# Transfers over all rows and a finer spread of weight decoding in the transform stage of a Fourier-filter kernel

## The chip, the cores and the metric

The kernel runs on one core of one Trainium2 chip. The metric is device time in microseconds (us) for one execution of the whole program, from inputs in device memory to the output in device memory. A single core has five engines that matter here: TensorE (PE) with its weight loads (PEld), VectorE (DVE), ScalarE (ACT), GpSimd (POOL) and SyncE (SP), which only issues transfers.

## The reference

A block filters a sequence in the frequency domain and sends the result through two gated layers:

```python
def _attn_ref(x, filt_r, filt_i):          # x: (2, 3008, 256)
    X = np.fft.rfft(x, axis=1)
    F = (filt_r + 1j * filt_i)[None, :, :]
    return np.fft.irfft(X * F, n=x.shape[1], axis=1).astype(np.float32)

def _moe_ref(x, w_gate, w_val, w_out):      # 256 -> 1536 -> 256
    g = x @ w_gate
    silu = g * (1.0 / (1.0 + np.exp(-g)))
    return (silu * (x @ w_val) @ w_out).astype(np.float32)

def _moe2_ref(x, w_in, w_out):              # 256 -> 2048 -> 256
    h = x @ w_in
    g = h * np.clip(h + 3.0, 0.0, 6.0) / 6.0
    return (g @ w_out).astype(np.float32)
```

All weights come as float64. The kernel gets them as pairs of 32-bit words and decodes them on the chip.

## The kernel before, in words

**The transform stage.** The length 3008 is split as 47 x 64, so a Fourier transform is two small matrix products. The 256 channels of the two batches are cut into 16 steps of 32 channels (the loop `for k in range(N + 2)` with N = 16). In step k stand, in this order on PE:

- n1(k), line 417: the product over the 47 rows of the input, 64 small matmuls, out of the buffer `xin`, into two PSUM banks. ACT copies the result to `first` (line 422).
- back(k-2), line 458: 32 matmuls that bring the filtered spectrum of two steps ago back over the 64 rows. ACT copies the result to `turned` (line 463).
- n2(k), line 431: 32 matmuls on `first[k]` over the 64 rows. It can't start before the copy of line 422.

After n2(k) comes the filter product: four operations on DVE (line 444), then two subtractions and two additions on POOL (lines 109 and 112 are the helpers `minus` and `plus`). For the first eight steps POOL also flips signs in the filter (line 409). Steps 16 and 17 hold back(14), back(15) and the first block's way back to time (`to_time`, line 157). The main stage follows: its first matmul is `l1` (line 246).

**Transfers.** All of them are issued by SP, in the program's order: input loads of two steps (`load_x`, line 381, one for each of the two row halves), filter loads (`load_filter`, line 384), raw weights (`Decode`, line 179), stores of the spectrum to `d2` (line 467, every fourth step, one for each half of the 128 rows) and the loads of `g` out of `d2` (line 140). The input has two buffers (tag `xs`) of two steps each, so the load of steps k+3 and k+4 is issued once n1(k) has read its buffer.

**Decoding.** A block of weights is decoded by one operation on ACT (`start`, line 184), three on DVE (`leading`, lines 192, 193, 195), and three more (`rest`, lines 202, 203 and an addition, line 112). Then ACT casts the word to its high part (`high_gv`, line 482, or line 530) and DVE subtracts for the low part (`low_gv`, line 485). In the transform stage three such blocks are decoded, `dec[0]`, `dec[1]` and `both`; the steps at which each part runs are written out by hand in the chain `if k == 5: ... elif k == 13`. Every engine runs its instructions in the order in which the program issues them. An ACT operation of the decoding that waits therefore holds back the copy to `first` of the next step, and with it n2 of that step.

**The main stage** goes over blocks of up to 512 tokens through both layers. Weights of the first layer are decoded on the way.

Of the kernel before, what the change touches and what calls it, by code (L numbers as in the profile page):

```python
# [16 lines left out]
P = 128  # L17
B, S, D = 2, 3008, 256
N1, N2 = 47, 64
N1P = 48  # L20
NK = 24
COLS = 8 * NK
DFF1, DFF2 = 1536, 2048
# [37 lines left out]
def _matrices():  # L61
# [11 lines left out]
    m[:, :NK, FIN:FIN + N1] = w * np.cos(a.T)  # L73
    m[:, NK:2 * NK, FIN:FIN + N1] = -w * np.sin(a.T)
# [4 lines left out]
def fft_conv_glu_mlp(ctx: ExitStack, tc: tile.TileContext, x, filt, mats, sgn, w1, w2, out):  # L79
# [21 lines left out]
    d2 = [dram.tile([2 * NK, N2, D], F32, name=f"d2_{b}") for b in range(B)]  # L101
# [67 lines left out]
    class Decode:  # L169
# [16 lines left out]
        def leading(self):  # L186
            if self.w is None:
                self.w = self.pool.tile([P, self.n], F32, tag="ww", name="ww")
            v, a, wu = nc.vector, self.a, self.w.bitcast(U32)
            au, high = a.bitcast(U32), self.raw[:, :, 1]  # L190

            v.tensor_scalar(out=a, in0=a, scalar1=LEAST, scalar2=MOST, op0=ALU.max, op1=ALU.min)
            v.tensor_scalar(out=wu, in0=au, scalar1=3, scalar2=0x3FFFFFF8,
                            op0=ALU.logical_shift_left, op1=ALU.bitwise_and)
            v.scalar_tensor_tensor(out=wu, in0=high, scalar=0xC0000000, in1=wu,
                                   op0=ALU.bitwise_and, op1=ALU.bitwise_or)

        def rest(self, engine=None):
            v, a, w = nc.vector, self.a, self.w
            au, wu, low = a.bitcast(U32), w.bitcast(U32), self.raw[:, :, 0]  # L200

            v.tensor_scalar(out=au, in0=wu, scalar1=0xFF800000, scalar2=None, op0=ALU.bitwise_and)
            v.scalar_tensor_tensor(out=a, in0=low, scalar=2.0 ** -52, in1=a, op0=ALU.mult, op1=ALU.mult)  # L203
            plus(w, w, a, engine or nc.gpsimd)
# [157 lines left out]
    with tc.manual_schedule():  # L362
# [13 lines left out]
        def load_x(k, n):  # L376
# [73 lines left out]
        def back(k):  # L450
# [35 lines left out]

        gt, xsd = {}, {}
        for k in range(N + 2):
# [13 lines left out]
            if k == 5:  # L502
                load_gv(0)
            elif k == 6:
                load_gv(1)
                dec[0].start()
            elif k == 7:
                dec[0].leading()
            elif k == 8:
                dec[0].rest(nc.vector)  # L510
                high_gv(0)
                dec[1].start()
            elif k == 9:
                low_gv(0)
                both = Decode(None, w1[:, 0:2, 1024:], 512,
                              (words(side[:, 1024:2048]), side[:, 2048:2560], dec[0].a))
                dec[1].leading()
            elif k == 10:
                dec[1].rest(nc.vector)
                high_gv(1)  # L520
                both.start()
            elif k == 11:
                low_gv(1)
                both.leading()
            elif k == 12:
# [306 lines left out]
```

## Time and profile before

| | us |
|---|---|
| median of 3 runs | 1233.47 |
| lowest, highest | 1231.89, 1237.01 |
| the profiled execution's own time | 1232.24 |
| its span in the trace | 1230.5 |
| busy PE / PEld / DVE | 1177.9 / 1044.3 / 1006.1 |
| busy ACT / POOL | 606.0 / 161.0 |

The table is to be read with care: a share of busy time is an average over a short stage at the start, in which PE is often idle, and a long one after it, in which PE is nearly always busy. The trace has the instructions by engine and time, what each engine waited for, and the transfers.

### The profile page before, as it was taken

To read this page: it belongs to the slowest core of one execution; us is meant where nothing else is said; L and a number is where in the kernel's file an instruction comes from. 1 tells how busy PE (TensorE), PEld (TensorE's weight loads), DVE (VectorE), ACT (ScalarE), POOL (GpSimd) and SP (SyncE) were. 2 spreads that over 40 slices of the span, in tenths; PEclk is the share of its full clock that TensorE was granted. 3 is DMA by queue.
4 is the path that set the end of the run, shared out by engine and by line. 5 is a ranking of instruction groups with operands and counts; after the bars stand their busy time and mean duration, and the time that the engine had idled before them with its cause. 6 is when DMAs were issued, how large, how long until landed. Compare 5 with 4: busy or idle time off the path is not lost.

```text
span 1230.5 us, 22770 instructions
## 1 busy us (share of the span) xinstructions
PE 1177.9 (96%) x9544; PEld 1044.3 (85%) x9544; DVE 1006.1 (82%) x1565; ACT 606.0 (49%) x897; POOL 161.0 (13%) x166
## 2 busy tenths in 40 slices
PE   6667999999999999999999999999999999999997
PEld 5656778888889988888888989999899999999997
DVE  2355888666577888877888899999999999999997
ACT  2223444444334444444444556666666666666664
POOL 3433244000000222201122320000000000000000
PEclk9888999999999999999999999999999999999999
DMA  8775530110011323121210310110011001101000
GB/s 191 159 167 115 135 103 26 55 23 18 17 38 52 84 80 104 35 85 41 68 52 16 111 62 1 35 35 8 28 33 35 6 28 35 35 1 35 33 18 16
DMA packets 35031, 68.28 MB, mean 55 GB/s; under 512 B 2832, under 2 KB 18832, under 8 KB 34256
## 3 DMA queue, kind: packets, MB, share of 16 engines
q1 hardware_dynamic: 34928, 66.82, 19.8%
q8 instruction: 75, 1.23, 0.4%
q14 instruction: 28, 0.23, 0.1%
HBM read 44.53 MB, written 22.28 MB: 54 GB/s over the span
## 4 chain that ended last, share of the span: by engine, by line
PE 88%; DVE 5%; DMA 3%; issue 2%; ACT 1%; SPq 1%; DVEq 0%
PE gv L246 51%; PE a L255 31%; PE a L121 2%; DMA side<-w_in 2%; PE a L431 1%; PE gv L157 1%; PE gv L458 1%; DMA xin<-x_in 1%; DVE hs L109 1%; DVE us L444 1%; PE gv L417 1%; SPq L467 1%; DVE h L109 0%; DVE x L203 0%; DVE h L765 0%
## 5 line engine op out<-in xcount | busy, mean ns | idle before, releaser
L255 PEld LDWEIGHTS a<-hs,wall 128*128 128x128 f32 x3276 | 408.3, 189 | 14.1 <-issue 1.2
L255 PE MATMUL a<-hs,wall 128*128 128x256 f32 (+1 forms) x3276 | 414.2, 282 | 1.8 <-issue 0.8
L246 PE MATMUL gv<-xs,wall 128*128 128x512 f32 (+1 forms) x1728 | 407.4, 391 | 1.4 <-ACT xs L608 1.2
L246 PEld LDWEIGHTS gv<-xs,wall 128*128 128x128 f32 x1728 | 320.8, 188 | 67.4 <-ACT xs L608 1.3
L109 DVE TENSOR_TENSOR hs<-h,hs 128x768 fp32r<-128x768 f32 (+2 forms) x324 | 350.6, 1082 | 30.0 <-ACT hs L302 18.1
L246 PE MATMUL gv<-xs,wi 128*128 128x512 f32 (+1 forms) x1152 | 276.0, 388 | 0.0
L246 PEld LDWEIGHTS gv<-xs,wi 128*128 128x128 f32 x1152 | 210.0, 188 | 37.1 <-DVE xs L109 0.4
L313 ACT CAST hs<-h 128x1024 fp32r<-128x1024 f32 (+1 forms) x156 | 160.8, 1031 | 116.3 <-DVE h L109 116.1
L302 ACT CAST hs<-h 128x768 fp32r<-128x768 f32 (+1 forms) x156 | 128.1, 821 | 150.6 <-PE a L255 95.1
L109 DVE TENSOR_TENSOR h<-h 128x512 f32<-128x512 f32 (+3 forms) x312 | 185.4, 594 | 6.8
L615 DVE TENSOR_TENSOR h<-h,gv 128x512 f32<-128x512 f32 (+1 forms) x144 | 96.8, 673 | 62.2 <-PE gv L246 58.1
L764 ACT ACTIVATE h<-gv 128x512 f32<-128x512 f32 (+1 forms) x192 | 109.8, 589 | 69.1 <-PE gv L246 51.1
L765 DVE SCALAR_TENSOR_TENSOR h<-h,gv 128x512 f32<-128x512 f32 (+1 forms) x192 | 129.1, 672 | 15.4 <-ACT h L764 10.4
L599 ACT ACTIVATE h<-gv 128x512 f32<-128x512 f32 (+1 forms) x144 | 84.7, 588 | 85.7 <-PE gv L246 84.3
L444 DVE TENSOR_TENSOR us<-a,x 128x384 f32<-128x384 f32 x64 | 31.5, 550 | 62.7 <-PE a L431 60.4
L112 POOL TENSOR_TENSOR ww<-ww,wa 128x512 f32<-128x512 f32 x16 | 20.7, 1295 | 377.1 <-issue 194.6
L112 DVE TENSOR_TENSOR h<-h 128x256 f32<-128x256 f32 (+1 forms) x156 | 67.6, 433 | 2.1
L431 PE MATMUL a<-first,mat 64*64 64x192 f32 x512 | 33.4, 385 | 22.7 <-ACT first L422 22.7
L431 PEld LDWEIGHTS a<-first,mat 64*64 64x64 f32 x512 | 25.9, 160 | 26.8 <-ACT first L422 24.9
L121 PE MATMUL a<-hs,wall 128*128 128x512 f32 x144 | 36.9, 407 | 3.7 <-DVE hs L109 3.7
L121 PEld LDWEIGHTS a<-hs,wall 128*128 128x128 f32 x144 | 27.7, 193 | 11.1 <-DVE hs L109 4.6
L417 PE MATMUL gv<-mat,xin 48*64 48x48 f32 x1024 | 24.4, 236 | 11.6 <-issue 9.3
(93 smaller groups left out, 616.1 us busy)
## 6 DMA issues: line engine op xcount, KB each, us to landing
raw<-w_in SPq DMA_DIRECT2D x16, 512.0 KB, 4.2
x<-w_in SPq DMA_DIRECT2D x10, 768.0 KB, 4.0
d<-turned SPq DMA_DIRECT2D x8, 768.0 KB, 8.4
xin<-x_in SPq DMA_DIRECT2D x14, 384.0 KB, 9.1
yd<-y SPq DMA_DIRECT2D x10, 512.0 KB, 2.9
g<-yd SPq DMA_DIRECT2D x10, 512.0 KB, 3.9
y_out<-y SPq DMA_DIRECT2D x20, 256.0 KB, 2.3
wt<-wd SPq DMA_DIRECT2D x8, 448.0 KB, 3.4
```

What stands on the lines that cost most here:

```text
L109: (engine or nc.vector).tensor_tensor(out=out, in0=a, in1=b, op=ALU.subtract)
L112: (engine or nc.vector).tensor_tensor(out=out, in0=a, in1=b, op=ALU.add)
L121: nc.tensor.matmul(acc, w, v, start=first and i == 0, stop=last and i == 2)
L246: nc.tensor.matmul(acc[:, :n], w[:, r, k * P:(k + 1) * P], xs[:, v, k, :n], start=(r, v, k) == (0, 0, 0), stop=(r, k) == (1, 1))
L255: nc.tensor.matmul(acc[b][:, 256 * h:256 * h + nt], w[:, r, iw], hs[:, v, ih, :nt], start=first and h == 0 and v == 0 and r == 1, stop=las ...
L302: nc.scalar.copy(out=self.parts(0, 0, 3), in_=v(1, 4))
L313: nc.scalar.copy(out=self.parts(0, 3, 7), in_=self.values(4, 8))
L431: nc.tensor.matmul(accs[o][rows(r), part * COLS:(part + 1) * COLS].rearrange("p (c q) -> p c q", q=NK), mat[rows(o), w:w + N2], f[rows(o), ...
L599: nc.scalar.activation(out=h, in_=hid[p].halves(gate), func=AF.Silu)
L615: nc.vector.tensor_tensor(out=h, in0=h, in1=hid[p].halves(val), op=ALU.mult)
L764: nc.scalar.activation(out=h, in_=pre, func=AF.Relu, bias=3.0)
L765: nc.vector.scalar_tensor_tensor(out=h, in0=h, scalar=6.0, in1=pre, op0=ALU.min, op1=ALU.mult)
```

## The change

It has four parts. The input is laid out so that one load brings two steps of both row halves, over 112 rows (47 rows of data and one of zeros, 16 unused rows, 48 rows again), and the loads are issued on ACT's queue. The filter is laid out so that the load of one step is contiguous. The store to `d2` takes all 128 rows at once; the rows of `d2` are ordered otherwise, and two lines of the matrix constants follow. The decoding in the transform stage is cut into six parts a block, of which two are run in a step (from a table `todo`); the raw words are loaded at steps 3, 5 and 10 in place of 5, 6 and 9, and the last addition of a block runs on POOL in place of DVE.

```diff
+XR = 64 + N1P
...
-    m[:, :NK, FIN:FIN + N1] = w * np.cos(a.T)
-    m[:, NK:2 * NK, FIN:FIN + N1] = -w * np.sin(a.T)
+    m[:, 0:2 * NK:2, FIN:FIN + N1] = w * np.cos(a.T)
+    m[:, 1:2 * NK:2, FIN:FIN + N1] = -w * np.sin(a.T)
...
-    d2 = [dram.tile([2 * NK, N2, D], F32, name=f"d2_{b}") for b in range(B)]
+    d2 = [dram.tile([NK, P, D], F32, name=f"d2_{b}") for b in range(B)]
...
-            nc.sync.dma_start(out=g[rows(r, N1P), :t1 - t0], in_=d2[b][:, 32 * r + t0:32 * r + t1])
+            nc.sync.dma_start(out=g[rows(r, N1P), :t1 - t0],
+                              in_=d2[b].rearrange("q (h n) c -> (q h) n c", h=2)[:, 32 * r + t0:32 * r + t1])
...
+        def part(self, i, engine=None):
...
+            if i == 0:
+                v.tensor_scalar(out=a, in0=a, scalar1=LEAST, scalar2=MOST, op0=ALU.max, op1=ALU.min)
...
+            elif i == 4:
+                v.scalar_tensor_tensor(out=a, in0=low, scalar=2.0 ** -52, in1=a, op0=ALU.mult, op1=ALU.mult)
+            else:
+                plus(w, w, a, engine or nc.gpsimd)
...
-            for r in range(2):
-                nc.sync.dma_start(out=xin[k // 2][rows(r, N1P), k % 2:k % 2 + n], in_=x[b, r, :, j:j + n])
+            nc.scalar.dma_start(out=xin[k // 2][:XR, k % 2:k % 2 + n], in_=x[b, j // 2, :, j % 2:j % 2 + n])
...
-            nc.sync.dma_start(out=fl[:, j], in_=filt[:, j])
+            nc.sync.dma_start(out=fl[:, j], in_=filt[j])
...
-                for h in range(2):
-                    nc.sync.dma_start(out=d2[b][h * NK:(h + 1) * NK, :, a * P:(a + 1) * P].rearrange("q n c -> n q c"),
-                                      in_=turned[rows(h), a])
+                nc.sync.dma_start(out=d2[b][:, :, a * P:(a + 1) * P].rearrange("q p c -> p q c"), in_=turned[:, a])
...
+        def load_both():
+            dec["o"] = Decode(None, w1[:, 0:2, 1024:], 512, (words(side[:, 1024:2048]), side[:, 2048:2560], dec[0].a))
...
+        todo = {3: [lambda: load_gv(0)], 5: [lambda: load_gv(1)], 6: [lambda: dec[0].start()]}
+        k = 7
+        for f in (0, 1, "o"):
+            for i in (0, 2, 4):
+                todo.setdefault(k, []).extend([lambda f=f, i=i: dec[f].part(i), lambda f=f, i=i: dec[f].part(i + 1)])
+                k += 1
+            if f == "o":
+                todo[k - 1].append(high_o1)
+                todo[k] = [lambda: low_o1(0), lambda: low_o1(1)]
+            else:
+                todo[k - 1] += [lambda f=f: high_gv(f)]
+                todo[k] = [lambda f=f: low_gv(f)]
+                todo[k] += [load_both, lambda: dec[1].start()] if f == 0 else [lambda: dec["o"].start()]
...
-            if k == 5:
-                load_gv(0)
-            elif k == 6:
-                load_gv(1)
-                dec[0].start()
-            elif k == 7:
-                dec[0].leading()
-            elif k == 8:
-                dec[0].rest(nc.vector)
-                high_gv(0)
-                dec[1].start()
...
+            for step in todo.get(k, ()):
+                step()
+            if k == N - 4:
                 dec[2] = decode_w1(2)
                 gt[0] = load_g(0, 0)
...
-    xt = np.zeros((B, 2, N1P, 8, 1024), f32)
...
+    xt = np.zeros((B, 4, P, 2, 1024), f32)
...
+    xt = xt[:, :, :XR]
```

In the table `todo`, the cast to the high part of the three blocks (`high_gv(0)`, `high_gv(1)`, `high_o1`) stands at steps 9, 12 and 15; before, it stood at steps 8, 10 and 12. The operation on ACT that starts a block stands at steps 6, 10 and 13; before, at 6, 8 and 10.

**ACT's order.** The rows are of ACT; `y<-side` and `wq<-side` start the first and the second block, `wall<-y` casts the first. Before, from step 6 to step 9:

```order
L184 ACTIVATE y<-side 128x512
L422 COPY first<-gv 128x384 x2
L463 COPY turned<-gv 128x24x16 x2
L422 COPY first<-gv 128x384 x2
L463 COPY turned<-gv 128x24x16 x2
L482 CAST wall<-y 128x512
L184 ACTIVATE wq<-side 128x512
L422 COPY first<-gv 128x384 x2
```

The same engine with the change, from step 9 to step 11 (the start of the first block stands three steps ahead of this piece):

```order
L432 COPY first<-gv 128x384 x2
L391 DMA xin<-x_in 112x2048
L473 COPY turned<-gv 128x24x16 x2
L490 CAST wall<-y 128x512
L432 COPY first<-gv 128x384 x2
L473 COPY turned<-gv 128x24x16 x2
L186 ACTIVATE wq<-side 128x512
L432 COPY first<-gv 128x384 x2
```

The cast of a block and the start of the next one no longer stand together but a step apart, and ACT now issues the input loads, between the two pairs of copies.

**SP's order.** The rows are the transfers from the last filter load to the words of the third block. Before:

```order
L384 DMA x_100<-filt_in 128x768
L381 DMA xin<-x_in 48x2048 x2
L467 DMA d_0_72<-turned 64x24x128 x2
L179 DMA side<-w_in 128x1024 x2
L381 DMA xin<-x_in 48x2048 x4
L467 DMA d_0_72<-turned 64x24x128 x2
L179 DMA side<-w_in 128x2x512
```

With the change, from the first filter load on:

```order
L394 DMA x_100<-filt_in 128x768 x8
L181 DMA side<-w_in 128x1024
L476 DMA d_0_72<-turned 128x24x128
L181 DMA side<-w_in 128x1024
L476 DMA d_0_72<-turned 128x24x128
L181 DMA side<-w_in 128x2x512
L181 DMA x_100<-w_in 128x1536
```

The words of the first block now stand ahead of the first store, those of the second behind it; the input loads have left this queue.

**DVE's order** around the first block (`us` is the filter product, `wall<-y,wall` the low part). Before:

```order
L195 SCALAR_TENSOR_TENSOR y<-side,y 128x512
L444 TENSOR_TENSOR us<-a,x_100 128x384 x4
L202 TENSOR_SCALAR y<-y 128x512
L203 SCALAR_TENSOR_TENSOR y<-side,y 128x512
L112 TENSOR_TENSOR y<-y 128x512
L444 TENSOR_TENSOR us<-a,x_100 128x384 x4
```

With the change:

```order
L200 SCALAR_TENSOR_TENSOR y<-side,y 128x512
L203 TENSOR_SCALAR y<-y 128x512
L454 TENSOR_TENSOR us<-a,x_100 128x384 x4
L205 SCALAR_TENSOR_TENSOR y<-side,y 128x512
L454 TENSOR_TENSOR us<-a,x_100 128x384 x4
L110 TENSOR_TENSOR wall<-y,wall 128x512
```

Ahead of the cast one operation of DVE is left behind the filter product where there were three; the addition has gone to POOL. From the main stage on, the order of every engine is the same in both.

## Rows read from the trace of the kernel before

**Rows 1.** Stretches: start:end, length, busy us by engine, granted PE clock, DMA share, GB/s.
```profile
0.00:43.80 43.80, 30.05 (x815) 27.18 (x819) 11.90 (x24) 10.96 (x24) 18.16 (x33) 0.92 0.78 173
43.80:108.30 64.50, 40.92 (x1157) 37.47 (x1152) 34.84 (x58) 18.47 (x43) 25.73 (x39) 0.84 0.70 148
108.30:118.00 9.70, 7.53 (x199) 6.90 (x190) 2.75 (x7) 2.79 (x6) 3.85 (x7) 0.82 0.50 134
118.00:1230.50 1112.50, 1099.39 (x7390) 972.78 (x7388) 956.66 (x1479) 573.78 (x824) 113.21 (x89) 1.00 0.15 45
```

**Rows 2.** PE's order in time: start, length, instruction, idle before and its releaser.
```profile
16.32 0.45 PE L417 MATMUL gv<-mat,xin 48*64 48x48 f32 x16 [1.82 <-DMA xin<-x_in]
...
28.03 1.57 PE L431 MATMUL a<-first,mat 64*64 64x192 f32 x32
31.66 1.48 PE L431 MATMUL a<-first,mat 64*64 64x192 f32 x32
...
43.78 1.48 PE L431 MATMUL a<-first,mat 64*64 64x192 f32 x32
...
54.55 2.88 PE L431 MATMUL a<-first,mat 64*64 64x192 f32 x30 [6.60 <-ACT first L422]
...
60.04 1.46 PE L431 MATMUL a<-first,mat 64*64 64x192 f32 x29
...
68.27 2.88 PE L431 MATMUL a<-first,mat 64*64 64x192 f32 x30 [3.95 <-ACT first L422]
...
85.53 2.89 PE L431 MATMUL a<-first,mat 64*64 64x192 f32 x30 [7.97 <-ACT first L422]
...
99.60 2.88 PE L431 MATMUL a<-first,mat 64*64 64x192 f32 x30 [3.06 <-ACT first L422]
...
108.29 1.62 PE L431 MATMUL a<-first,mat 64*64 64x192 f32 x32
```

**Rows 3.** Waits from 0 to 125: engine, line, releaser: total us, times, longest.
```profile
ACT y L184 <- DMA side<-w_in: 8.6, 1, 8.6
...
ACT wall L530 <- DVE y L112: 6.4, 1, 6.4
ACT wall L482 <- DVE sm L112: 6.3, 1, 6.3
ACT wall L482 <- DVE y L112: 5.4, 1, 5.4
...
ACT side L184 <- DMA side<-w_in: 2.6, 1, 2.6
```

**Rows 4.** The same view, PE's waits for its own instructions.
```profile
PE gv L417 <- issue: 9.3, 6, 3.2
...
PE gv L458 <- issue: 2.2, 1, 2.2
```

**Rows 5.** DVE and POOL in order of time, step 8.
```profile
62.05 1.94 DVE L444 TENSOR_TENSOR us<-a,x 128x384 f32<-128x384 f32 x4
...
65.68 0.96 DVE L112 TENSOR_TENSOR y<-y 128x512 f32<-128x512 f32 x1
...
65.06 1.03 POOL L112 TENSOR_TENSOR us<-us 128x192 f32<-128x192 f32 x1
```

**Rows 6.** Groups of instructions: count, busy us, mean ns, idle before.
```profile
L112 POOL TENSOR_TENSOR ww<-ww,wa 128x512 f32<-128x512 f32 x16 | 20.7, 1295 | 377.1 <-issue 194.6
...
L184 ACT ACTIVATE wq<-side 128x512 f32<-128x512 f32 x1 | 0.7, 652 | 0.0
```

**Rows 7.** Transfers: 5.5 to 16 in all; stores and input loads, SP's issue (min/median/max ns).
```profile
DMA packets 700, 2.39 MB, mean 228 GB/s; under 512 B 117, under 2 KB 117, under 8 KB 603
...
d<-turned SPq DMA_DIRECT2D x8, 768.0 KB, 8.4
...
L381 SPq DMA_DIRECT2D xin<-x_in x18: 310/426/1665, 1.2 to 77.0; - x18
```

More of the change, by code (lines that the diff above doesn't have):

```diff
@@ L198, in rest @@
-        def rest(self, engine=None):
[L199 to L204, printed above, removed]
+            v, a, w = nc.vector, self.a, self.w
+            au, wu, low, high = a.bitcast(U32), w.bitcast(U32), self.raw[:, :, 0], self.raw[:, :, 1]
@@ L206, in word, with leading @@
+        def leading(self):
+            for i in range(3):
+                self.part(i)
+        def rest(self, engine=None):
+            for i in range(3, 6):
+                self.part(i, engine)
         def word(self, engine=None):
@@ L485, in low_gv, with high_o1, low_o1 @@
             minus(wgv[:, f, 1], dec[f].w, wgv[:, f, 0].bitcast(F32))
-        gt, xsd = {}, {}
+        def load_both():
+            dec["o"] = Decode(None, w1[:, 0:2, 1024:], 512, (words(side[:, 1024:2048]), side[:, 2048:2560], dec[0].a))
+        def high_o1():
+            for r in range(2):
+                o = wo1[:, 0, 0, 0:4:3] if r == 0 else wo1[:, 0, 0, 1:3]
+                nc.scalar.copy(out=o, in_=dec["o"].w.rearrange("p (r a c) -> p r a c", r=2, c=P)[:, r])
+        def low_o1(r):
+            hi, lo = (wo1[:, 0, h, 0:4:3] if r == 0 else wo1[:, 0, h, 1:3] for h in range(2))
+            minus(lo, dec["o"].w.rearrange("p (r a c) -> p r a c", r=2, c=P)[:, r], hi.bitcast(F32))
+        gt, xsd = {}, {}
+        todo = {3: [lambda: load_gv(0)], 5: [lambda: load_gv(1)], 6: [lambda: dec[0].start()]}
[11 more added lines that the diff above has]
+                todo[k] += [load_both, lambda: dec[1].start()] if f == 0 else [lambda: dec["o"].start()]
         for k in range(N + 2):
@@ L501, in fft_conv_glu_mlp @@
                 filter_product(k)
-            if k == 5:
-                load_gv(0)
-            elif k == 6:
-                load_gv(1)
-                dec[0].start()
-            elif k == 7:
-                dec[0].leading()
-            elif k == 8:
-                dec[0].rest(nc.vector)
-                high_gv(0)
-                dec[1].start()
[L513 to L525, printed above, removed]
-                both.rest(nc.vector)
-                o = [[wo1[:, 0, h, 0:4:3] if r == 0 else wo1[:, 0, h, 1:3] for h in range(2)] for r in range(2)]
-                bw = both.w.rearrange("p (r a c) -> p r a c", r=2, c=P)
-                for r in range(2):
-                    nc.scalar.copy(out=o[r][0], in_=bw[:, r])
+            for step in todo.get(k, ()):
+                step()
+            if k == N - 4:
                 dec[2] = decode_w1(2)
                 gt[0] = load_g(0, 0)
-            elif k == 13:
-                for r in range(2):
-                    minus(o[r][1], bw[:, r], o[r][0].bitcast(F32))
             elif k == N:
@@ L542, in fft_conv_glu_mlp @@
                     split(*time_halves(xsd[0], block, 0, r))
[L543 removed]
+        del dec[0], dec[1], dec["o"]
         n_pair = n_block * G1
@@ L797 @@
     x = np.asarray(inputs["x"])
[L798 to L801 removed]
+    xt = np.zeros((B, 4, P, 2, 1024), f32)
+    for r in range(2):
+        xt[:, :, 64 * r:64 * r + N1] = (x[:, time].reshape(B, N1, N2, 4, 2, 2, 16)[:, :, :, :, :, r]
+                                        .transpose(0, 3, 1, 4, 5, 2).reshape(B, 4, N1, 2, 1024))
+    xt = xt[:, :, :XR]
+    ft = np.stack([np.asarray(inputs[name])[row].reshape(NK, N2, 8, 2, 16).transpose(2, 3, 1, 4, 0).reshape(8, P, 2 * COLS)
                    for name in ("filt_r", "filt_i")], axis=2)
```

19 lines of the change are left out of this document (8 added, 11 removed).

## The prediction, before the run

> **What bounds the kernel now.** I read the stretches first. From 118 us on PE is busy for 1099.4 of 1112.5 us at full granted clock [rows 1]. The change leaves the order there as it is, so I keep those 1112.5 us. What can be won lies ahead of them, in the transform stage, where PE stands still for about a third of the time: 30.1 of 43.8 us busy up to n2(6), 40.9 of 64.5 us from n2(6) to n2(15).
>
> Then PE's order in time. Two n2 that follow each other without a wait start 31.66 - 28.03 = 3.63 us apart [rows 2]: this is a natural step. Nine of them, from n2(6) at 43.78 to n2(15) at 108.29, would take 32.7 us; they take 64.5. Four waits for ACT's copy to `first` make 6.60 + 3.95 + 7.97 + 3.06 = 21.6 us of the difference. Each also slows what follows: the n2 behind the wait lasts 2.88 us where another lasts 1.48, and the next n2 starts 60.04 - 54.55 = 5.49 us later instead of 3.63. That is 1.86 us a wait, 7.4 in all. It is the granted clock, which is 0.84 on the mean of this stretch [rows 1], between the two levels of 2.4 GHz and 1.2 GHz.
>
> Then the waits say why the copy was late. ACT sat in front of an operation of the decoding: 8.6 us for the words of the first block, 5.4, 6.3 and 6.4 us for DVE before the three casts, 2.6 us for the words of the third block [rows 3]. The copy to `first` stands behind it on ACT. So of the four waits of PE the first is a late transfer, the second and the fourth are casts that wait for DVE, and the third is a cast and a transfer together.
>
> **The change part by part: the late words.** The words of the first block are loaded at step 3 and no longer behind a store; they are needed at step 6. Those of the second block have five steps from issue to use (18 us of natural steps), those of the third at least three (steps 10 to 13, with a cast wait among them, some 17 us). The store ahead of each of the latter landed 8.4 us after issue in halves [rows 7]. I take all three as in time: the 8.6 and the 2.6 us go.
>
> **The casts.** Here the spread does less than it says. In step 9 the last two parts of block 0 and its cast still stand together, and the cast stands ahead of `first[10]`. I build the step from rows. n2(9) takes 1.48 us. The filter product then starts; in step 8 it started at 62.05, and POOL's last operation of it ended at 65.06 + 1.03 = 66.09, 4.04 us later [rows 5]. The addition, now on POOL and behind that, costs 1.30 (the same form in the main stage [rows 6]). In step 8 the addition ended at 65.68 + 0.96 = 66.64 and n2(9) started at 68.27, 1.63 us later; 0.65 of that was the start of the next block, which moves away [rows 2, 5, 6], so 0.98 is left. From n2(9) to n2(10) that is 1.48 + 4.04 + 1.30 + 0.98 = 7.80 us, a wait of 4.2 us. The saving of two DVE operations ahead of the cast is eaten by POOL's queue. The same comes at step 12. At step 15 no `first` stands behind the cast.
>
> The nine steps are then: 6 to 9, 3 x 3.63 = 10.9; 9 to 10, 7.80; 10 to 11, 5.49; 11 to 12, 3.63; 12 to 13, 7.80; 13 to 14, 5.49; 14 to 15, 3.63; together 44.7 us. PE also waits for its own instructions ("issue") six times for 9.3 us in n1 over 16 steps [rows 4], 0.58 a step. Long waits for ACT covered some of these before, so I give all nine steps their share: 5.2 us. The sum is 49.9, against 64.5: **14.6 us less**. Bounds for the instructions: none seen (0), or the longest wait of 3.2 us in each of the six steps that no wait covers (19.2).
>
> **DVE and POOL in the other steps.** Two parts of a block come behind the product, 1.94 + 2 x 0.96 at most = 3.9 us a step on DVE [rows 5], at most 0.2 above a natural step. In the five such steps that is 1 us at most, within the range.
>
> **Input loads on ACT.** A load costs the issuing engine 0.43 us, at most 1.67 [rows 7]. On ACT it stands behind the copies to `first`, which n2 needs, and ahead of those to `turned`, whose banks back needs only a step later, 3.6 us. So it is hidden even at 1.67; without that cover it would cost at most 1.67 in each of six steps, 10 us. The load of steps 4 and 5 now waits on ACT for the load of steps 2 and 3; `first[2]` is queued behind it, and needs that load anyway. I put it at nothing.
>
> **Filling at the start.** SP's queue no longer has input in it, so all eight filter loads and the first block's words are issued without regard to the steps. The input of steps 0 to 3 is 4 x 112 x 4 KB = 1.84 MB. Before, its last part landed at about 16.3 us, where n1(2) waited for it [rows 2]. The rate from 5.5 to 16 us was 228 GB/s [rows 7]. If bytes are shared by row length (8 KB against 3 KB of filter), 2.5 MB go by in 11 us, and with about 2 us ahead of the first byte landing is no longer the limit: up to 2 us won. If they are shared in halves, 3.7 MB take 16.1 us, so about 18 us, 2 us lost, and the load of steps 4 and 5, issued after it, may cost another 1.5. Between -2 and +3.5 I take **1.0 us more**.
>
> The Trainium skill, "DMA: Bandwidth & Descriptors", section "Issuing engines are not separate DMA queues", says that transfers of several issuing engines run on the same 16 DMA engines and interleave, and that only issue time is saved. By that rule the second queue wins no bandwidth and the late end holds, which would put the sum at 1223.1; the trace before has all data on one queue and can't show it.
>
> **Store, filter, padding.** The store moves the same bytes in one transfer; nothing on PE waited for it, and SP, which issues it, is not on the path: nothing. The padding adds 16 rows to 96, a sixth of the input bytes; it is counted below as a rival. A contiguous filter may load faster; the step that follows is bound by the input, so I count nothing, between -1 and +1.
>
> **The end of the stage.** At step 15 the cast waits until 1.48 + 4.04 + 1.30 = 6.8 us after n2(15), and the copies of back(14), the split of the first block and two low parts on DVE come after it. The way from n2(15) to the main stage took 9.7 us [rows 1] and hides most: **0.7 us more**, between 0 and 2.
>
> **Sum.** 1232.24 - 14.6 + 1.0 + 0.7 = 1219.3 us against the profiled execution's own time. The median of the runs is 1.23 above that, so the forecast is **1220.6 us**. A difference within 0.5% (6.2 us, so 1227.3 to 1239.6) could not be told from none.
>
> **The rivals.**
>
> *The transfers become the bound.* From 43.8 to 108.3 us they filled 0.70 of 64.5 us, 45.2 us at full share [rows 1]. The padding of six steps adds 0.39 MB or 1.7 us at 228 GB/s, the first block's words (0.5 MB) leave, -2.3. That is 44.6 us of work for a stretch of 49.9. For it: the early stretch, full of transfers, only reached a share of 0.78, and at that the nine steps take 57.2, 7.3 more: 1227.9 us. Against it: the input loads, the only ones with a short term, no longer stand behind stores. Chance 0.12.
>
> *PE waits for instructions instead.* With the long waits gone, each of six uncovered steps shows the longest such wait: 19.2 - 5.2 = 14 us more, 1234.6 us, no change. For it: such waits stood in steps where nothing else held PE. Against it: six waits in 16 steps had a mean of only 1.55. Chance 0.06.
>
> *Slower.* At steps 10 and 14 ACT's copies to `turned` overwrite what the first and the second store read. The first store is issued near 40 us, and n2(10) comes at 43.8 + 10.9 + 7.8 = 62.5, so it has 22 us. Rows of 512 B compete with input rows of 8 KB; if the engines took one row of each queue in turn, the store would stand nearly still during two loads of 0.92 MB, 4 us each: about 8.4 + 8 = 16.4, still in time. It decides from 22 us on. At 34 us each of the two steps waits 12 + 1.9 us, 27.8 us in all: 1248.4 us. Chance 0.05.
>
> *Better than forecast.* The input is in time from the start (-2 where I took +1) and the waits for instructions keep to a few (2 us of 5.2): 6.2 us less, 1214.4 us; with a cast that waits 2 us less at both places, 1210.4. Chance 0.15.
>
> **How the numbers follow.** The forecast keeps 0.60, with its own range of 1214 to 1227; 0.02 is left for the change doing nothing (1233.5). The range of 1209 to 1231 holds the forecast, the better case and the transfers as the bound, and leaves out the other cases and the ends of the bounds. Faster by over 0.5%: the forecast, the better case and some of the transfer rival, 0.80. Within 0.5%: the rest of that one, the instructions and no effect, 0.15. Slower: 0.05.
>
> **What would show it.** The waits of ACT for the raw words (8.6 and 2.6) are gone. PE's n2 shows two waits of about 4 us for ACT, at steps 10 and 13, in place of four, with ACT's casts waiting for POOL; n2(6) to n2(15) is about 50 us. The main stage starts near 105 us and lasts 1112 as before. I am wrong if n1 waits for input after step 4, if ACT's copies to `turned` wait for a store, if PE's waits for instructions pass 10 us, or if the main stage's length moves by more than 3 us.

## The result, and the profile after

The changed kernel takes 1214.34 us in the median (1210.82 to 1216.00), the kernel before in the same comparison 1232.68 us (1231.49 to 1237.01): a ratio of 0.9841 [0.9808, 0.9874], 18.3 us less. The profiled execution is the fastest of its four: 1210.82 us, with a span of 1208.5 us against 1230.5. So the two traces below differ by 22.0 us, some 4 us more than the medians do. A trace is one execution, and those of one kernel lie 5 to 7 us apart (one below from 1212.03 to 1219.47); verdicts below on a whole kernel go by ratios, and a stretch of a trace only says where the time lies.

The stretches of the changed kernel, cut at the same places as [rows 1] (n2(6), n2(15), the first matmul of the main stage); columns as there:

```profile
0.00:38.77 38.77, 28.61 (x812) 27.36 (x816) 11.15 (x23) 10.95 (x24) 17.29 (x31) 0.91 0.77 220
38.77:85.85 47.08, 36.55 (x1159) 34.26 (x1153) 28.80 (x51) 18.03 (x41) 28.32 (x40) 0.93 0.76 212
85.85:95.94 10.09, 6.17 (x201) 5.12 (x191) 6.57 (x12) 3.35 (x9) 6.79 (x9) 1.00 0.56 149
95.94:1208.50 1112.56, 1100.82 (x7388) 974.22 (x7388) 956.45 (x1479) 573.25 (x824) 113.38 (x89) 1.00 0.14 44
```

The way up to n2(6) is 5.0 us shorter (38.77 against 43.78), the nine steps from n2(6) to n2(15) 17.4 us (47.08 against 64.51), the end of the stage 0.4 us longer, the main stage the same. That is all of the 22.0 us.

PE's order in time, the changed kernel (n1 is now line 427, n2 line 441):

```profile
17.35 0.85 PE L427 MATMUL gv<-mat,xin 48*64 48x48 f32 x43 [1.81 <-issue]
...
24.53 0.85 PE L427 MATMUL gv<-mat,xin 48*64 48x48 f32 x44 [1.75 <-issue]
...
31.70 1.57 PE L441 MATMUL a<-first,mat 64*64 64x192 f32 x32
...
35.24 1.57 PE L441 MATMUL a<-first,mat 64*64 64x192 f32 x32
...
38.77 1.57 PE L441 MATMUL a<-first,mat 64*64 64x192 f32 x32
...
41.43 0.92 PE L427 MATMUL gv<-mat,xin 48*64 48x48 f32 x49 [0.87 <-issue]
...
45.97 0.96 PE L427 MATMUL gv<-mat,xin 48*64 48x48 f32 x50 [0.80 <-issue]
...
50.95 0.95 PE L427 MATMUL gv<-mat,xin 48*64 48x48 f32 x49 [1.23 <-issue]
...
53.01 1.57 PE L441 MATMUL a<-first,mat 64*64 64x192 f32 x32
...
60.78 2.88 PE L441 MATMUL a<-first,mat 64*64 64x192 f32 x30 [3.78 <-ACT first L432]
...
70.65 1.58 PE L441 MATMUL a<-first,mat 64*64 64x192 f32 x32
...
74.67 0.96 PE L427 MATMUL gv<-mat,xin 48*64 48x48 f32 x51 [2.34 <-issue]
...
78.51 1.74 PE L441 MATMUL a<-first,mat 64*64 64x192 f32 x30 [1.51 <-ACT first L432]
...
85.85 1.62 PE L441 MATMUL a<-first,mat 64*64 64x192 f32 x32
```

In place of the four waits for ACT's copy [rows 2] there are two, at n2(10) and n2(13). The waits up to 110 us, same kernel (engine, line, releaser: total us, times, longest):

```profile
PE gv L427 <- issue: 8.8, 6, 2.3
...
PE a L441 <- ACT first L432: 6.4, 4, 3.8
ACT wall L501 <- POOL y L113: 6.4, 1, 6.4
ACT wall L490 <- POOL sm L113: 5.6, 1, 5.6
ACT wall L490 <- POOL y L113: 5.6, 1, 5.6
```

ACT no longer waits for raw words (8.6 and 2.6 us in [rows 3]). Its three casts still wait, for POOL's addition now and no longer for DVE. The first of them in the order of POOL and then of ACT:

```profile
58.44 1.26 POOL L113 TENSOR_TENSOR y<-y 128x512 f32<-128x512 f32 x1
```

```profile
59.73 0.62 ACT L490 CAST wall<-y 128x512 fp32r<-128x512 f32 x1 [5.63 <-POOL y L113]
```

The addition ends at 59.70, the cast starts at 59.73, and n2(10) starts at 60.78.

The queues of the changed kernel, over the whole execution (packets, MB, share of 16 engines):

```profile
q10 hardware_dynamic: 1152, 7.34, 2.3%
q8 instruction: 74, 1.21, 0.4%
```

The input has a queue of its own, q10. The other row matters in what follows: the profile counts the loads of an engine's instructions on the same 16 DMA engines as data. The 74 loads of q8 bring 1.21 MB, 16 KB each, and PE has 2 x 9544 = 19,088 instructions with its weight loads: 258 a load. A step of the transform stage has 2 x (64 + 32 + 32) = 256, so about one load a step. That PE's waits named "issue" are waits for these loads shows in the times of the packets: in n1 up to 110 us the 13 traces that have such waits show 72 of them, and each ends 1.2 to 1.7 us after the end of a load of q8. In each that is longer than 2.5 us, the load began only after PE had stopped.

### The profile page after: what moved, and what is told of

It is laid out like the page before. It is cut to its first block, busy times and chain, and to the rows that moved or that the text cites. A ratio compares the mean times of both kernels' runs of the same rounds, so it can differ in the third digit from the quotient of the medians.

```text
span 1208.5 us, 22740 instructions
## 1 busy us (share of the span) xinstructions
PE 1172.1 (97%) x9544; PEld 1040.9 (86%) x9544; DVE 1003.0 (83%) x1562; ACT 605.6 (50%) x897; POOL 165.8 (14%) x169
## 3 DMA queue, kind: packets, MB, share of 16 engines
q10 hardware_dynamic: 1152, 7.34, 2.3%
q8 instruction: 74, 1.21, 0.4%
## 4 chain that ended last, share of the span: by engine, by line
PE 90%; DVE 5%; DMA 2%; issue 1%; ACT 1%; POOL 1%; SPq 0%; DVEq 0%; POOLq 0%
PE gv L257 52%; PE a L266 31%; PE a L122 2%; PE gv L159 1%; PE a L441 1%; PE gv L468 1%; PE gv L427 1%; DVE hs L110 1%; DMA d<-turned 1%; DVE us L454 1%; DVE h L110 0%; DMA g<-d 0%; DMA mat<-mats_in 0%; DVE h L769 0%; DVE x L205 0%
## 5 line engine op out<-in xcount | busy, mean ns | idle before, releaser
L441 PE MATMUL a<-first,mat 64*64 64x192 f32 x512 | 29.4, 352 | 6.4 <-ACT first L432 6.4
L432 ACT COPY first<-gv 128x384 f32<-128x384 f32 x32 | 13.8, 481 | 36.6 <-PE gv L427 36.6
```

The costliest lines, as they stand in the source:

```text
L441: nc.tensor.matmul(accs[o][rows(r), part * COLS:(part + 1) * COLS].rearrange("p (c q) -> p c q", q=NK), mat[rows(o), w:w + N2], f[rows(o), ...
```

## The experiments

The letters in an expectation stand for the theories as they are told in that expectation. Every ratio is against the kernel before, run on the same chip. The changed kernel was run a second time: 1213.47 us (1210.73 to 1214.67), ratio 0.9830 [0.9808, 0.9852], n2(6) at 39.23 and n2(15) at 86.81 us. So it repeats.

> The changed kernel once more, on the chip of the next three: 1210 to 1217 us, the waits of PE for its own instructions in n1 between 7 and 14 us up to the main stage.

### One part at a time

**The decoding alone**: the changed kernel with input, filter, store and the rows of the matrices as before (cut to the input).

```diff
-            nc.scalar.dma_start(out=xin[k // 2][:XR, k % 2:k % 2 + n], in_=x[b, j // 2, :, j % 2:j % 2 + n])
+            for r in range(2):
+                nc.sync.dma_start(out=xin[k // 2][rows(r, N1P), k % 2:k % 2 + n], in_=x[b, r, :, j:j + n])
...
```

> The kernel before with the new spread of the decoding alone; input, filter and stores as before, all on SP. Theory A (the gain lies in where the decoding stands on ACT): n2(6) to n2(15) falls from 64.5 to about 48 us, n2(6) stays near 43.8, median about 1216 to 1219. Theory B (the gain lies in the transfers: on one queue, input and words stand behind stores): n1 at steps 8 to 14 or ACT at steps 10 and 13 waits for transfers by 8 us or more, n2(6) to n2(15) stays above 55 us, median 1223 to 1229.

Measured 1223.02 us (1221.39 to 1223.40), ratio 0.9902 [0.9887, 0.9917]: 11.4 us of the gain. n2(6) comes at 44.50 us, the nine steps take 54.3. The words were in time, n1 waits for input only at step 2, as before, and of the two cast waits one shows, of 4.05 us for a forecast of 4.2. Something else filled the steps, in the view of the waits up to 110 us and in PE's order:

```profile
PE gv L426 <- issue: 17.2, 6, 4.5
```

```profile
49.90 0.96 PE L426 MATMUL gv<-mat,xin 48*64 48x48 f32 x50 [3.71 <-issue]
...
87.20 1.75 PE L426 MATMUL gv<-mat,xin 48*64 48x48 f32 x57 [4.54 <-issue]
```

In n1, PE waits 17.2 us for its own instructions, against 9.3 before [rows 4] and 8.8 in the changed kernel.

**The transfers alone**: the changed kernel, with the hand-written chain of decoding steps of before.

```diff
-            for step in todo.get(k, ()):
-                step()
+            if k == 5:
+                load_gv(0)
+            elif k == 6:
+                load_gv(1)
+                dec[0].start()
...
```

> The changed kernel with the old steps of the decoding (words loaded at steps 5, 6 and 9, three operations a step, the addition on DVE). Theory A: n2(6) comes near 39 us as in the changed kernel, the waits of ACT for words (8.6 us before) and for DVE before the casts stay, n2(6) to n2(15) is 60 us or more, median 1225 to 1231. Theory B: the words come in time without the new steps too, n2(6) to n2(15) falls to 50 to 54 us, median 1215 to 1221.

Measured 1222.00 us (1216.93 to 1223.01), ratio 0.9884 [0.9857, 0.9911]: 12.4 us, where I had priced the transfers at a loss of 1.0. n2(6) comes at 38.40 us, so the early gain is theirs. The nine steps keep the old waits and take 62.3 us:

```profile
PE a L441 <- ACT first L432: 19.7, 6, 5.5
```

The two parts alone add up to 23.8 us, against 18.3 and 20.6 for both in its two comparisons.

### Which of the transfers it is

**Input on SP's queue again**, all else changed.

```diff
-            nc.scalar.dma_start(out=xin[k // 2][:XR, k % 2:k % 2 + n], in_=x[b, j // 2, :, j % 2:j % 2 + n])
+            nc.sync.dma_start(out=xin[k // 2][:XR, k % 2:k % 2 + n], in_=x[b, j // 2, :, j % 2:j % 2 + n])
```

> The changed kernel with the input loads (still 112 rows, two steps in one) issued by SP. Theory A: the nine steps from n2(6) keep about 47 to 50 us, since the input comes in time from either queue; what is lost is at the start only: n2(6) back at 41 to 44 us, median 1214 to 1219. Theory B (the own queue carries it): SP, in order, holds an input load behind a store that waits for ACT, n1 waits for input by 3 us or more at steps 8, 10, 12 or 14, median 1220 or more.

Measured 1217.36 us (1214.91 to 1217.54), ratio 0.9854 [0.9839, 0.9869]. The interval overlaps those of the changed kernel, so the whole time doesn't tell them apart, but the start does: n2(6) is back at 43.03 us. PE's order there:

```profile
23.96 0.85 PE L427 MATMUL gv<-mat,xin 48*64 48x48 f32 x44 [3.71 <-issue]
...
35.96 1.51 PE L427 MATMUL gv<-mat,xin 48*64 48x48 f32 x45 [4.53 <-issue]
```

The same two steps of the kernel before, with the wait ahead of them:

```profile
17.71 1.42 PE L417 MATMUL gv<-mat,xin 48*64 48x48 f32 x43 [0.94 <-issue]
...
26.07 0.85 PE L417 MATMUL gv<-mat,xin 48*64 48x48 f32 x44 [3.15 <-issue]
...
36.51 0.92 PE L417 MATMUL gv<-mat,xin 48*64 48x48 f32 x49 [3.17 <-issue]
```

In the changed kernel the first is 1.75 us and the second is gone: its n2 start 3.54 us apart from 31.70 to 38.77. (In its second trace the first is 3.17 us, and the second is gone too.) Over all runs with n1 as it is and with all of its input, n2(6) comes at 38.4 to 40.7 us in the eight that load both halves at once on ACT's queue, and at 43.0 to 44.5 us in the three that load on SP's. PE's waits for instructions up to there add up to 2.6 to 5.2 us in the eight and to 7.2 to 9.3 us in the three.

**The filter as before**, all else changed.

```diff
-            nc.sync.dma_start(out=fl[:, j], in_=filt[j])
+            nc.sync.dma_start(out=fl[:, j], in_=filt[:, j])
```

> The changed kernel with the filter laid out as before (rows of 3 KB, 24 KB apart). If the contiguous filter is what lifts the rate from 10 to 20 us (316 to 337 GB/s after, 176 to 293 before), the rate falls back below 290 GB/s, filter and input land later, and n2(6) comes 2 us or more later than the 38.8 to 39.2 of the changed kernel: 1215 to 1218. If the rate comes from the second queue, nothing moves: 1211 to 1216.

Measured 1214.27 us (1212.03 to 1219.47), ratio 0.9850 [0.9831, 0.9869]: no difference. (Its profiled execution is the slowest of the five; its nine steps take 53.6 us, so one trace of them can be 6 us off.) The rows from 10 to 20 us (columns as in [rows 1]) show where the input's rate comes from; first the kernel before, then the changed one, then input on SP, then the old filter:

```profile
10.00:20.00 10.00, 6.12 (x173) 5.18 (x175) 4.00 (x8) 1.53 (x4) 6.42 (x10) 0.87 1.03 234
```

```profile
10.00:20.00 10.00, 7.58 (x225) 6.81 (x229) 4.00 (x8) 2.10 (x5) 5.49 (x9) 0.93 1.03 327
```

```profile
10.00:20.00 10.00, 8.41 (x261) 7.79 (x257) 4.00 (x8) 2.58 (x6) 6.41 (x10) 1.00 1.02 288
```

```profile
10.00:20.00 10.00, 7.59 (x251) 6.69 (x248) 4.09 (x8) 2.76 (x7) 6.01 (x10) 1.00 1.04 345
```

The DMA engines are at full share in all four. With one queue they move 234 and 288 GB/s, with two 327 and 345, with either filter layout. So, with both halves in one load, the second queue raises the rate, and the layout of the filter doesn't; the way from 234 to 288 comes with the larger loads or the filter. With loads of one half the second queue does not raise it, as the next run shows.

**Two loads of 48 rows each on ACT's queue** in place of one of 112 rows.

```diff
-            nc.scalar.dma_start(out=xin[k // 2][:XR, k % 2:k % 2 + n], in_=x[b, j // 2, :, j % 2:j % 2 + n])
+            for r in range(2):
+                nc.scalar.dma_start(out=xin[k // 2][rows(r, N1P), k % 2:k % 2 + n],
+                                    in_=x[b, j // 2, 64 * r:64 * r + N1P, j % 2:j % 2 + n])
```

> The changed kernel with each input load issued as two of 48 rows, still on ACT, so without the 16 unused rows: a seventh fewer input bytes, twice the issues on ACT. If the padding costs, the stretch from n2(6) gets up to 2 us shorter and the median falls by 1 to 2 us; if the issue on ACT (0.32 us each) costs, the copies to turned come later by 0.3 us and nothing else moves. I expect within 2 us of the changed kernel.

Measured 1219.71 us (1217.46 to 1221.95), ratio 0.9890 [0.9867, 0.9913]: 0.5 to 0.6% above the changed kernel's two ratios, some 6 to 7 us, where I expected no more than 2. The padding is not the price; the loads in halves are. ACT's order at the start:

```profile
0.73 10.21 ACTq L392 DMA_DIRECT2D xin<-x_in  x6
...
10.98 1.28 ACT L408 ACT_TABLE_LOAD   x1 [10.98 <-DMA x<-filt_in]
```

ACT is busy with six issues until 10.94 us, and the profile names a filter load as what released it, which the input has nothing to do with. (In the changed kernel, too, an issue of a filter load on SP waits 2.5 us, by the profile for the landing of an input load.) n2(6) comes at 43.44 us, and the nine steps take 49.7. I take it that the two transfers share a completion semaphore; no run took that apart. The rate from 10 to 20 us is that of the kernel before, although the input has its own queue and the DMA engines are at full share:

```profile
10.00:20.00 10.00, 6.00 (x130) 5.01 (x130) 2.47 (x5) 3.09 (x6) 2.79 (x5) 0.83 1.04 229
```

**The store in halves of 64 rows**, all else changed.

```diff
-                nc.sync.dma_start(out=d2[b][:, :, a * P:(a + 1) * P].rearrange("q p c -> p q c"), in_=turned[:, a])
+                for h in range(2):
+                    nc.sync.dma_start(out=d2[b][:, rows(h), a * P:(a + 1) * P].rearrange("q p c -> p q c"),
+                                      in_=turned[rows(h), a])
```

> The changed kernel with each store to d2 issued as two of 64 rows. The bytes and the rows of 512 B are the same and SP is not waited for, so I expect no difference: 1211 to 1216 us. If fewer, larger stores carry part of the gain, ACT or PE's instruction loads wait longer beside the halves and the median is 1217 or more.

Measured 1217.52 us (1217.17 to 1221.87), ratio 0.9894 [0.9872, 0.9916], 0.5 to 0.6% above the changed kernel's two ratios, or 6 to 8 us; the interval lies above that of the second run and touches that of the first, and it lies above that of the old filter (0.9850), run on the same chip. I had expected nothing. The start is kept (n2(6) at 39.06), the nine steps take 54.3 us, and PE's order shows two long waits:

```profile
49.79 1.63 PE L427 MATMUL gv<-mat,xin 48*64 48x48 f32 x50 [4.36 <-issue]
...
82.52 1.63 PE L427 MATMUL gv<-mat,xin 48*64 48x48 f32 x51 [5.91 <-issue]
```

In n1 PE waits 14.6 us for instructions, against 8.8 and 10.1 in the two traces of the changed kernel. But the second long wait has no store beside it: what moves from 70 us until its end is input, raw words and the loads of `g`. How two stores come to cost this is not shown.

### What holds the nine steps now

**Each cast one step later**, with the low part behind it, so that it no longer waits for POOL.

```diff
-                todo[k - 1].append(high_o1)
-                todo[k] = [lambda: low_o1(0), lambda: low_o1(1)]
+                todo[k] = [high_o1, lambda: low_o1(0), lambda: low_o1(1)]
...
-                todo[k - 1] += [lambda f=f: high_gv(f)]
-                todo[k] = [lambda f=f: low_gv(f)]
+                todo[k] = [lambda f=f: high_gv(f), lambda f=f: low_gv(f)]
```

> The changed kernel with the three casts to the high part moved one step later, behind the next copies to first. Theory A (the two waits that are left, 3.78 and 1.51 us, come from the cast standing ahead of the copy): both go, with 1 to 2 us of slow clock behind the first, n2(6) to n2(15) falls from 47.1 to 40 to 43 us, median 1208 to 1211. Rival C (the wait is only passed on: PE runs into waits for its own instructions or for input, or DVE, with 1.95 + 1.0 + 1.5 us a step, becomes the bound): n2(6) to n2(15) stays at 45 us or more, median 1212 to 1215.

Measured 1209.99 us (1207.95 to 1210.88), ratio 0.9796 [0.9782, 0.9811], less than the changed kernel's 0.9830 and 0.9841, with intervals that just meet. The two waits at the casts are gone, and yet the nine steps take 47.3 us, as in the changed kernel: waits for instructions took their place. (The trace is of the slowest of four executions here and of the fastest there, so the stretch may hide a gain that the ratio shows.)

```profile
PE gv L427 <- issue: 13.9, 7, 3.7
```

```profile
74.07 1.63 PE L427 MATMUL gv<-mat,xin 48*64 48x48 f32 x51 [3.71 <-issue]
```

This last wait runs from 70.36 to 74.07. The transfers of this kernel just ahead of it, from 66.0 to 70.3 us (a line of totals, then packets, MB and share by queue), and then those from 70.3 to 74.1:

```profile
DMA packets 170, 1.06 MB, mean 246 GB/s; under 512 B 26, under 2 KB 26, under 8 KB 86
...
q10 hardware_dynamic: 94, 0.69, 66.0%
q1 hardware_dynamic: 76, 0.37, 37.9%
```

```profile
DMA packets 80, 0.33 MB, mean 86 GB/s; under 512 B 30, under 2 KB 30, under 8 KB 74
...
q1 hardware_dynamic: 68, 0.27, 33.5%
q10 hardware_dynamic: 11, 0.04, 4.6%
q8 instruction: 1, 0.02, 2.3%
```

While input and other data fill the engines, from 66.0 to 70.3, no instruction load moves. One does from 71.27 to 72.67, as the other queues run out, and PE goes on 1.40 us after its end. That is one place and an order in time; the next two runs take away either side of it.

**No input loads after step 3**, on the kernel with the later casts.

```diff
+            if k >= 4:
+                xin[k // 2] = xin[k // 2 % 2]
+                return
```

> e4_cast_a_step_later without the input loads of steps 4 to 15: n1 reads the input of steps 0 to 3 again, so the output is of other data; 5.5 MB of transfers are left out. Theory D: with the queues shorter the instruction loads land earlier, the waits called issue fall from 13.9 us to 5 us or less, n2(6) to n2(15) to 35 to 39 us, against 32.7 for natural steps. Rival E (the waits come from PE's pace alone): they stay at 10 us or more and the stretch at 44 us or more.

Measured 1201.84 us (1197.96 to 1205.72), ratio 0.9739 [0.9694, 0.9784]. The waits:

```profile
PE gv L430 <- issue: 6.3, 2, 3.2
```

They fall from 13.9 us in 7 to 6.3 us in 2. These two, of 3.16 and 3.15 us, follow stretches in which SP's queue alone fills the DMA engines, the first with a store and raw words, the second with raw words and the loads of `g`. n2(6) comes at 34.86 us, 3.9 us sooner than with the later casts, and the nine steps take 44.8 us, 2.5 us less. I had expected 35 to 39 us: less data takes away more than half of the waits, but the nine steps give back only a small part.

**Half the instructions in n1**, on the kernel with the later casts: 32 matmuls of 128 columns in place of 64 of 64, so 192 instructions a step.

```diff
-                for o in range(2):
-                    for r in range(2):
-                        nc.tensor.matmul(accs[r][rows(o), c * N1P:(c + 1) * N1P],
-                                         t[rows(r, N1P), k % 2, (o * 8 + c) * N2:(o * 8 + c + 1) * N2],
-                                         mat[rows(r, N1P), M1:M1 + N1P])
+                for r in range(2):
+                    nc.tensor.matmul(accs[r][:, c * N1P:(c + 1) * N1P], t[rows(r, N1P), k % 2, c * P:(c + 1) * P],
+                                     mat[rows(r, N1P), M1:M1 + N1P])
```

> e4_cast_a_step_later with n1 done by 32 matmuls of 128 columns a step in place of 64 of 64 (the input's columns laid out for it): a step has 192 PE instructions with their weight loads instead of 256, and the same columns to stream. Theory D (the waits called issue are loads of PE's own instructions, which take their turn among the data on the DMA engines, and now bound a step): fewer instruction loads, n2(6) to n2(15) falls from 47.3 us to 41 to 44 us, the waits from 13.9 to under 9 us, median 1203 to 1208. Rival E (the waits are not tied to the amount of instructions, or the wider matmuls run half as many side by side): the stretch stays at 46 us or more, median 1209 to 1213.

Measured 1211.52 us (1209.42 to 1214.77), ratio 0.9820 [0.9793, 0.9847], no gain on the later casts alone. But the waits for instructions in n1 are gone, and the nine steps take 43.2 us, 4.1 us less than with the later casts and as theory D had it. The group of n1 from 40 to 90 us (count, busy us, mean ns, idle before), here and then with 64 columns:

```profile
L426 PE MATMUL gv<-mat,xin 48*128 48x48 f32 x332 | 20.8, 274 | 0.0
```

```profile
L427 PE MATMUL gv<-mat,xin 48*64 48x48 f32 x576 | 12.8, 226 | 11.1 <-issue 11.1
```

What was won is spent ahead of the nine steps. Up to n2(6) and from there to n2(15), columns as in [rows 1]:

```profile
0.00:49.36 49.36, 42.48 (x588) 37.22 (x592) 11.70 (x24) 10.95 (x24) 19.27 (x35) 1.00 0.61 182
49.36:92.56 43.20, 42.64 (x871) 38.19 (x864) 29.93 (x52) 18.38 (x41) 28.36 (x40) 1.00 0.84 233
```

n2(6) comes 10.6 us later than with the later casts. n1 of one step is busy for 20.8 / (332 / 32) = 2.0 us where it was 12.8 / (576 / 64) = 1.4, and a step without a wait takes 4.68 us (n2 at 49.36 and 54.04) where it took 3.54. Besides, n1(0) to n1(2) are busy for 3.65 us each and only from n1(3) on for 1.99; why the start is that slow stays open, for the granted clock of the row reads 1.00.

### Towards a faster kernel

**The matrices first, on ACT's queue**, on the kernel with the later casts: in the changed kernel they land at 5.45 us, before at 2.97.

```diff
-        nc.sync.dma_start(out=mat, in_=mats)
+        nc.scalar.dma_start(out=mat, in_=mats)
```

> e4_cast_a_step_later with the load of the matrices issued on ACT ahead of the input, no longer on SP beside it. In the changed kernel it landed at 5.5 us, before at 3.0. It should land near 3 us again, n1(0) starts 2 us earlier; if input or filters bound the next steps, n2(6) keeps its 38.7 us and the median is that of e4 (1210); if not, n2(6) comes 1 to 2 us earlier and the median is 1208 to 1209.

Measured 1208.94 us (1207.82 to 1212.28), ratio 0.9821 [0.9799, 0.9842]: no gain. The matrices land at 3.19 us, but now n1(0) waits 1.24 us for input, and n2(6) comes at 40.66.

**Fewer instructions where wide matmuls cost less**: on top of that, the back transform in 8 matmuls of 384 columns a bank, and two terms of n2 in one; 208 instructions a step.

```diff
-            for m, (h, w, part) in enumerate(((0, CO, 0), (1, CO, 1), (1, SI, 0), (0, NS, 1))):
+            for r in range(2):
+                for o in range(2):
+                    nc.tensor.matmul(accs[o][rows(r), :2 * COLS].rearrange("p (h c q) -> p h c q", h=2, q=NK),
+                                     mat[rows(o), CO:CO + N2], f[rows(o), r], start=True, stop=False)
+            for h, w, part in ((1, SI, 0), (0, NS, 1)):
...
-            for o in range(2):
-                for m in range(2):
-                    for h in range(2):
...
-                                             u[rows(r), o, part], start=(o, m) == (0, 0), stop=(o, m) == (1, 1))
+            for m in range(2):
+                for h in range(2):
...
+                                         mat[rows(r), w:w + N2], u[rows(r), :, part], start=m == 0, stop=m == 1)
```

> e10_matrix_first with back done by 8 matmuls of 384 columns in place of 16 of 192, and the two of n2's four terms that share their weights done as one: 208 PE instructions a step in place of 256, the same columns streamed and the same number side by side. Theory D (instruction loads, behind data, bound a step): n2(6) to n2(15) falls from 47.3 us to 40 to 44, the waits called issue in the stage from 13.9 us to 9 or less, median 1202 to 1207. Rival F (other waits take their place, of n1 for input or of n2 for ACT): the waits for instructions fall, but the stretch stays at 45 us or more, median 1208 to 1210.

Measured 1207.01 us (1204.57 to 1209.24), ratio 0.9800 [0.9780, 0.9820]. The nine steps take 43.0 us, against 48.1 us with the matrices first, and n1 from 40 to 85 us waits less than half of the 11.1 us with the later casts alone:

```profile
L427 PE MATMUL gv<-mat,xin 48*64 48x48 f32 x576 | 12.2, 218 | 5.2 <-issue 5.2
```

Up to 110 us n1 waits 9.4 us, against 14.6 with the matrices first; I had expected 9 or less. This trace is of the fastest of four executions and the one with the matrices first of the slowest, so the two stretches differ by more than the kernels may. By the ratio it can't be told from the later casts alone (0.9796), nor from the matrices first (0.9821). Both take 2.0% less than the kernel before, and both have lower ratios than the changed kernel (0.9841 and 0.9830), with intervals that meet or overlap at the edge. Up to 105 us it has 15 instruction loads, against 18 with the later casts and 13 with half of n1.

## Why the prediction was right, and where it was not

The forecast of 1220.6 us was 6.3 us above the median, inside the range, at the lower end of the likeliest case's own (1214 to 1227). On the profiled execution, the fastest of its four, the parts of the sum put the main stage at 105.1 us and it starts at 95.94: some 6 us of that lie at the start and 2.8 in the nine steps. Step by step, on that execution:

- **The main stage stays**: forecast 1112.5 us, measured 1112.56. Right.
- **The late words go**: the 8.6 and 2.6 us are gone. Right.
- **The casts keep their wait**: n2(9) to n2(10) was forecast at 7.80 us, through POOL's queue; it took 60.78 - 53.01 = 7.77. n2(12) to n2(13) took 78.51 - 70.65 = 7.86, but in another way: a wait of 2.34 us for instructions ahead of the copy, then 1.51 us for the copy itself. The two waits, which the sum had added up, shared one hole.
- **The clock behind a wait**: n2(10), behind its wait, lasts 2.88 us, and the next two steps take 70.65 - 60.78 = 9.87 us (forecast 5.49 + 3.63 = 9.12). n2(13) lasts 1.74 us for 30 matmuls, with a shorter wait ahead of it, and the two steps after it take 85.85 - 78.51 = 7.34. The slow stretch I had counted twice came once; the granted clock of the nine steps is 0.93, against 0.84 in [rows 1].
- **Waits for instructions in the nine steps**: forecast 5.2 us, measured 0.87 + 0.80 + 1.23 + 2.34 = 5.24, of which the last lies in the cast's hole. So the nine steps took 47.1 us for a forecast of 49.9: 2.3 for that hole and 1.8 for the clock behind n2(13), less some 1.2 that the other steps took more.
- **The end of the stage**: forecast 0.7 us more, measured 0.4. Right.
- **"Filling at the start" failed**: between -2 and +3.5 I took 1.0 us more; it was 5.0 us less (and 4.6 on the second trace). I had priced the landing of input alone. The waits of n1(2) for input (0.56 and 1.82 us) did go, and the matrices, which I did not look at, came 2.48 us later; these two cancel. What I left out were PE's waits for instructions up to n2(6): 0.94 + 3.15 + 3.17 = 7.26 us before, 1.81 + 1.75 = 3.56 after, and the slow clock behind the one at step 5. With input on SP they are back.
- **"Input loads on ACT" and "store": nothing** failed likewise. I looked for who waits for these transfers, and nobody does. But PE's instructions share the DMA engines with them. The input's place on its own queue is worth some 4 us of the way to n2(6), and one store in place of two 6 to 8 us of the whole; that the latter acts through the instruction loads is likely, not shown.
- **The rival "PE waits for instructions instead"** had the right mechanism and the wrong size: 8.8 us in n1 over all steps, 10.1 in the second trace. The second number is past the 10 us that were to show the forecast wrong, and yet the time stayed in its range: that sign was set too close to the 9.3 us of the kernel before. In the decoding alone it came true in good part (17.2 us and 54.3 us for the nine steps). The transfers, which I thought neutral, are what kept it small in the whole change. My two errors had opposite signs in the sum of the parts: the decoding alone gave 11.4 us where 13.9 were forecast, the transfers 12.4 us where a loss of 1.0 was. These errors don't cancel; the whole stayed in the range because the two parts together won less than their sum.
- **The rival "better than forecast"** named 1214.4 us, and the median is 1214.34. That is luck: it took 2 us off the start and 2 us for the waits for instructions in the nine steps, and the trace shows 5.0 and 5.24.
- **The transfers as the bound, and a store too late for its buffer**: neither n1 behind input after step 4 nor a wait of the copies to `turned` for a store shows. Rightly low.

The Trainium skill, "DMA: Bandwidth & Descriptors", section "Issuing engines are not separate DMA queues", by which the sum was 1223.1, did not hold here in its consequence: the transfers share the engines, as it says, but with both halves in one load two queues moved 327 GB/s where one moved 288, and n2(6) came some 4 us sooner. With loads in halves the traces agree with it: two queues moved 229 where one moved 234. The Trainium skill, "DMA: Bandwidth & Descriptors", section "Rules for kernel authors", says to use one transfer over 128 partitions in place of two over halves, and the runs agree: with the store in halves the kernel was 6 to 8 us slower. And the Trainium skill, "Runtime: NRT & Kernel Launch", section "Instruction fetch mechanics", says that instructions come in blocks of 16 KiB over a DMA queue of their own, at a cost that is mostly hidden; the trace agrees on the block (16 KB, 258 instructions), but in the transform stage the cost was not hidden: waits of up to 5.9 us.

What stays open is why the order in which data of two queues and of two halves are served leaves an instruction load behind them for so long: the runs show that fewer data, fewer instructions, one store in place of two and a second queue each shorten these waits, in one or two traces each, not by which rule.

## What to carry to other kernels

Where a profile shows "issue" waits on an engine with many short instructions beside heavy transfers, count instructions per step and look for the loads of instructions in the queues: a transfer that nobody waits for can still cost time by standing ahead of them. Price a change of transfers by that too, and don't add a wait for instructions to a wait that lies in the same hole. When a wait is taken off a step, name the next one in line: moving the casts took both of their waits away, and in the trace waits for instructions left the nine steps as long as they were. And look at the whole way: halving the instructions of n1 shortened the nine steps by 4.1 us and lengthened the start by 10.6.

## What the runs showed of the hardware

- PE's instructions came in loads of 16 KB, which the profile counts on the DMA engines that move data. n1, with 128 instructions in a step, waited for them for up to 5.9 us at a time, and each of 72 such waits ended 1.2 to 1.7 us after the end of a load.
- Two stores of 64 rows in place of one of 128, of the same bytes on the same queue, cost 6 to 8 us. The one trace of it has 14.6 us of waits for instructions in n1, against 8.8 and 10.1.
- At full share of all DMA engines the rate from 10 to 20 us was 234 GB/s with loads of 48 rows on one queue and 229 on two, 288 with loads of 112 rows on one and 327 or 345 on two.
- Half as many matmuls of twice the columns (274 ns for 226 in the mean) made a step without waits longer, 4.68 us for 3.54, and took the waits for instructions away.
- An engine that issues transfers can be held up: six issues took ACT 10.2 us, and the profile names the landing of a transfer of another engine's queue as what released it.
